# Loading the modulation's shift and scale apart, opening qkv by contraction block, one transpose by DMA, and a new instruction order

## The chip, the cores and the metric

The kernel runs on one NeuronCore of one Trainium2 chip. The metric is device time in microseconds (us) of that core, from runs without other load. A run's time is about 1.7 us longer than the profiled span of the same run, because the span counts from the first instruction to the last.

## The reference, cut

One transformer block whose two layer norms are scaled, shifted and gated by a conditioning vector. S = 2048 tokens, D = 512, 32 heads of 16, bf16.

```python
mod = (_silu(c) @ w_mod).reshape(c.shape[0], 6, 1, -1)
sa, ca, ga, sb, cb, gb = (mod[:, 0].copy(), ..., mod[:, 5].copy())   # 512 numbers each
h = _layernorm(x, axis=-1) * (1 + ca) + sa
x = x + ga * _A_ref(h, A_wqkv, A_wo)          # dilated local attention: window 8, dilation 2
h = _layernorm(x, axis=-1) * (1 + cb) + sb
x = x + gb * _B_ref(h, B_w_gate, B_w_up, B_w_down)   # gelu(h Wg) * (h Wu) @ Wd, Df = 1792
```

`w_mod` is 512 x 3072: its first 512 columns make the shift `sa`, the next 512 the scale `ca`. Nothing of the first qkv product can be computed before both are known.

## The kernel before

Every operation is first recorded in a plan, with its engine and its dependences. The plan is then emitted in one fixed order, the list `ORDER`, which was found beforehand by annealing on a model of the engines. So each engine runs its instructions in exactly that order: an operation whose input is late holds up everything behind it on its engine. Tokens go in five groups of 256, 256, 512, 512 and 512.

The loads that come first, and the two columns of the modulation. The 1 MB load brings shift (`b = 0`) and scale (`b2 = 1`) in one piece:

```python
    load_x(0, 2, -1000)
    load_cols(wm01, w_mod, 0, 2 * D, -999)          # shift and scale, 1 MB, one DMA
    load_cols(wqkv[0], A_wqkv, 0, D, -998)
    ...
        pe(0.41, lambda: cols(b, 0), r=[wm[b] or wm01, scT], w=[(mps, 0)], pri=p)     # shift: 16 matmuls of one column
        pe(0.41, lambda: cols(b2, 1), r=[wm[b2] or wm01, scT], w=[(mps, 1)], pri=p)   # scale
        act(0.09, lambda: nc.scalar.add(out=scl[:, off // 2:off // 2 + 4], in_=mps[:, 4:8], add=1.0), ...)
        act(0.09, lambda: nc.scalar.copy(out=modT[:, off:off + 4], in_=mps[:, 0:4]), ...)
```

Until the first qkv product can start, TensorE is kept busy with dummy matmuls on a tile named `warm` (14 of `warm_up`, then `filler`). How many `filler` matmuls go in is worked out from the gaps that the plan's model sees, so an edit can change their number (7 to 19 in these runs). The norm's output `xn` is transposed on TensorE into `tp` in PSUM, and ScalarE or VectorE applies scale and shift on the way to `hT` (the affine step). Where the tags are `None`, a DMA transpose writes the tile and ScalarE works on it in place:

```python
    LN1_TAGS = (("psL", "psB"), ("psF", "psF"), ("psF", "psF"), None, None)
    LN2_TAGS = (("psB", "psB"), None, None, None, None)
    ...
        if tags is None:
            ...  dq.dma_start_transpose(out=dst[...], in_=xn[...])      # one DMA for two token tiles
            for dt in range(DT):
                act(..., nc.scalar.activation(out=dst[:, 0:n // P, dt, :], in_=dst[:, 0:n // P, dt, :],
                    func=ACT.Identity, scale=scl[...], bias=modT[...]), ...)
```

The qkv product of one output tile, with the four contraction blocks `dt` innermost; the first tile waits for all of `hT[0]`:

```python
            def mm(b=b, j0=j0, ps=ps):
                for j in range(j0, j0 + nj):
                    for dt in range(DT):
                        nc.tensor.matmul(ps[:, j - j0, :], lhsT=wqkv[b][:, dt, j:D:4], rhs=h_cols(hT, g, dt),
                                         start=(dt == 0), stop=(dt == DT - 1))
```

The sums over a head's 16 dimensions and over the window ("folds", tiles `LT` and `o_ps`, `tile_position=(0, 32 * r)`), and the softmax sums `ss`, use the array in four column tiles; qkv, projection (`x_ps`), gate, up and down products (`g_ps`, `u_ps`, `y_ps`) use all of it. And the very last token tile is evicted in two halves, so that the last store is short:

```python
            parts = 2 if g == NG - 1 and c4 == n // P - 1 else 1
```

## Time and profile before

| | before |
|---|---|
| time, median (lowest to highest) | 246.88 us (246.49 to 247.17) |
| profiled span | 244.9 us |
| TensorE busy share | 97% |
| VectorE, ScalarE busy share | 67%, 62% |
| first qkv matmul starts | 13.34 us |
| first qkv tile and second group's transposes done | 14.66 us |
| last matmul ends | 241.44 us |

The last three rows cut the span into what happens before TensorE's real work is under way, the work itself, and the tail. They are read from TensorE's timeline. The prediction below shows the lines of the page, the stretches and the timeline that they come from.

How the views are read: a timeline or chain line begins with start and length in us, then the engine, the line of the kernel and the operation; `xN` counts instructions run together, and brackets hold the idle time before them and what ended it. A line of the waits view ends with total us, times, longest.

### The profile page before, as it was taken

The numbers are of one execution on the slowest core, as the hardware profiler recorded it, in microseconds if no ns is written. First come the engines' busy times: TensorE is split into PE (matmuls) and PEld (weight loads), VectorE is DVE, ScalarE is ACT, GpSimd is POOL, SyncE is SP. The second block draws the span as 40 slices with busy tenths as digits, with TensorE's granted clock in tenths as the row PEclk, the third lists the DMA queues.
The fourth block names the chain that finished last, engine by engine and source line by source line (L and its number), as shares of the span: only waits on it lengthen the run. The fifth ranks groups of instructions, "written<-read, shape, count | busy, mean of one in ns | idle before, by whom it ended". The sixth has DMA issues, their size and how long they took to land.

```text
span 244.9 us, 4342 instructions
## 1 busy us (share of the span) xinstructions
PE 237.5 (97%) x1691; PEld 129.1 (53%) x1691; DVE 164.8 (67%) x317; ACT 152.6 (62%) x280; POOL 22.2 (9%) x45
## 2 busy tenths in 40 slices
PE   7899999999999999999999999999999999999994
PEld 2489755457766534785444444444444444444452
DVE  3999999999995899799876746793432432121222
ACT  2089778988969729883657797157556816657300
POOL 1562012320000200110000001200000110000000
PEclk9999999999999999999999999999999999999998
DMA  6997979999799047592025090410000241000001
GB/s 188 355 305 209 186 180 288 183 248 361 234 215 217 0 131 170 141 220 43 1 60 138 0 186 12 86 64 2 3 0 0 43 88 66 0 0 0 3 24 62
DMA packets 37386, 28.84 MB, mean 118 GB/s; under 512 B 13045, under 2 KB 35958, under 8 KB 37366
## 3 DMA queue, kind: packets, MB, share of 16 engines
q1 hardware_dynamic: 37216, 28.56, 47.3%
q8 instruction: 13, 0.21, 0.4%
q14 instruction: 7, 0.06, 0.1%
q10 hardware_dynamic: 150, 0.00, 0.0%
HBM read 21.40 MB, written 4.28 MB: 105 GB/s over the span
## 4 chain that ended last, share of the span: by engine, by line
PE 79%; DVE 15%; POOL 2%; DMA 1%; issue 1%; ACT 1%; DVEq 0%; POOLq 0%
PE g_ps L786 20%; PE u_ps L786 19%; PE y_ps L813 17%; PE qkv_ps L598 10%; PE x_ps L763 6%; DVE pq L646 4%; DVE st L512 3%; PE o_ps L748 3%; DVE pv L732 3%; PE LT L656 2%; POOL rstd L518 2%; DVE xn L522 2%; DMA x_sg<-in_A_x_dram 1%; PE LT L686 1%; DVE mv L514 1%
## 5 line engine op out<-in xcount | busy, mean ns | idle before, releaser
L786 PE MATMUL g_ps<-h2T,Wg 128*128 128x512 bf16 (+1 forms) x280 | 54.4, 337 | 0.0
L786 PE MATMUL u_ps<-h2T,Wu 128*128 128x512 bf16 (+1 forms) x280 | 54.2, 337 | 0.0
L813 PE MATMUL y_ps<-WdP,hht 128*128 128x512 bf16 (+1 forms) x238 | 49.9, 367 | 0.5 <-DVE hht L798 0.5
L598 PE MATMUL qkv_ps<-hT,wqkv 128*128 128x512 bf16 (+1 forms) x240 | 45.7, 337 | 0.4 <-ACT hT L561 0.4
L795 ACT ACTIVATE gl<-g_ps 128x512 bf16<-128x512 f32 x56 | 33.0, 600 | 18.6 <-PE g_ps L786 17.3
L798 DVE TENSOR_TENSOR hht<-gl,ub 128x512 bf16<-128x512 bf16 x56 | 22.6, 422 | 32.4 <-ACT gl L795 20.4
L797 ACT CAST ub<-u_ps 128x512 bf16<-128x512 f32 x56 | 32.1, 590 | 12.8 <-PE u_ps L786 12.2
L786 PEld LDWEIGHTS <-Wg 128*128 128x128 bf16 x280 | 27.1, 98 | 22.9 <-issue 1.3
L786 PEld LDWEIGHTS <-Wu 128*128 128x128 bf16 x280 | 27.1, 98 | 22.1 <-issue 0.6
L813 PEld LDWEIGHTS <-hht 128*128 128x128 bf16 x238 | 23.1, 98 | 25.7 <-DVE hht L798 0.9
L598 PEld LDWEIGHTS <-wqkv 128*128 128x128 bf16 x240 | 25.7, 114 | 14.2 <-issue 2.2
L518 POOL TENSOR_TENSOR rstd<-rstd,neghalf 128x2 f32<-128x2 f32 x16 | 16.4, 1042 | 173.4 <-DVE rstd L507 143.3
L640 DVE TENSOR_TENSOR pq<-qT,kT 128x2048 bf16<-128x2048 bf16 x24 | 28.6, 1220 | 0.4
L732 DVE TENSOR_TENSOR pv<-e,vR 128x2048 bf16<-128x2048 bf16 x24 | 28.7, 1219 | 0.2
L534 ACT ACTIVATE h2T<-h2T,modT,scl 128x512 bf16<-128x512 bf16 (+1 forms) x16 | 11.1, 753 | 14.1 <-DMA h2T<-xn 14.1
L826 DVE TENSOR_TENSOR ot<-y_ps,x_sg 128x512 bf16<-128x512 f32 (+1 forms) x13 | 8.2, 648 | 14.5 <-PE y_ps L813 13.1
L763 PE MATMUL x_ps<-woP,oT 128*128 128x512 bf16 x64 | 15.8, 380 | 0.0
L767 DVE SCALAR_TENSOR_TENSOR x_sg<-x_ps,x_sg 128x512 bf16<-128x512 f32 x16 | 11.0, 685 | 6.3 <-PE x_ps L763 6.2
L504 ACT ACTIVATE xn<-x_sg,xsum 128x512 bf16<-128x512 bf16 x16 | 11.4, 718 | 3.3 <-DVE xsum L501 3.3
L512 DVE BATCH_NORM_STATS2 st<-x_sg 128x6 f32<-128x512 bf16 x16 | 10.3, 671 | 2.6 <-DMA x_sg<-in_A_x_dram 2.6
L754 ACT CAST oT<-o_ps 128x512 bf16<-128x512 f32 x16 | 9.0, 588 | 4.8 <-PE o_ps L748 4.8
L605 ACT CAST vT<-qkv_ps 128x512 bf16<-128x512 f32 x16 | 9.5, 592 | 3.7 <-PE qkv_ps L598 2.5
(92 smaller groups left out, 203.8 us busy)
## 6 DMA issues: line engine op xcount, KB each, us to landing
vR<-scr SPq DMA_DIRECT2D x24, 260.0 KB, 5.0
vR<-scr SPq DMA_DIRECT2D x8, 264.0 KB, 4.6
wm<-in_w_mod_dram SPq DMA_DIRECT2D x4, 512.0 KB, 5.2
out_dram<-ot SPq DMA_DIRECT2D x15, 128.0 KB, 1.7
Wg<-in_B_w_gate_dram SPq DMA_DIRECT2D x2, 896.0 KB
Wu<-in_B_w_up_dram SPq DMA_DIRECT2D x2, 896.0 KB, 8.1
WdP<-in_B_w_down_dram SPq DMA_DIRECT2D x2, 896.0 KB, 9.9
scr<-vT SPq DMA_DIRECT2D x6, 264.0 KB, 9.6
```

The source lines that it names most:

```text
L504: act(0.75, lambda i=i, xn=xn, nm=nm, mv=mv, c0=c0: nc.scalar.activation(out=xn[:, i, :], in_=x[g, c0 + i], func=ACT.Square, bias=nm[:, i: ...
L512: dve(0.59, lambda i=i, st=st, c0=c0: nc.vector.bn_stats(out=st[:, i, :], in_=x[g, c0 + i]), r=[x.key(g, c0 + i)], w=[(st, i)], pri=p)
L518: gp(0.65, lambda rstd=rstd: nc.gpsimd.tensor_tensor(out=rstd[:], in0=rstd[:], in1=neghalf[:, 0:2], op=ALU.pow), r=[rstd, neghalf], w=[rst ...
L598: nc.tensor.matmul(ps[:, j - j0, :], lhsT=wqkv[b][:, dt, j:D:4], rhs=h_cols(hT, g, dt), start=(dt == 0), stop=(dt == DT - 1))
L640: dve(1.14, lambda j=j, wg=wg, t=pq[m]: nc.vector.tensor_tensor(out=t[:], in0=_ap(q[g][:, j, 0:n], [[0, 4], [1, n]]), in1=_ap(k[g][:, j, : ...
L732: dve(1.14, lambda jj=jj, jl=jl, wg=wg, t=pv[m]: nc.vector.tensor_tensor(out=t[:], in0=_ap(e[:, wg, :], [[0, 4], [1, n]]), in1=vR[g][jj][: ...
L763: nc.tensor.matmul(x1_ps[:], lhsT=oT[:, j, c4 * P:(c4 + 1) * P], rhs=woP[:, j, :], start=(j == 0), stop=(j == 3))
L786: nc.tensor.matmul(ps[:, ft - f0, :], lhsT=Wt[ft // 7][:, dt, ft % 7 * P:(ft % 7 + 1) * P], rhs=h_cols(h2, g, dt), start=(dt == 0), stop=( ...
L795: act(0.485, lambda gl=gl, ps=gu[0]: nc.scalar.activation(out=gl[:], in_=ps[:], func=ACT.Gelu_apprx_tanh), r=[gu[0]], w=[gl], pri=p, table ...
L797: act(0.475, lambda ub=ub, ps=gu[1]: nc.scalar.copy(out=ub[:], in_=ps[:]), r=[gu[1]], w=[ub], pri=p)
L798: dve(0.335, lambda gl=gl, ub=ub, ht=ht: nc.vector.tensor_tensor(out=ht[:], in0=gl[:], in1=ub[:], op=ALU.mult), r=[gl, ub], w=[ht], pri=p)
L813: nc.tensor.matmul(y_ps[:], lhsT=hh[ft // nf][:, ft % nf, c4 * P:(c4 + 1) * P], rhs=WdP[:, ft, c0:c0 + w], start=(ft == 0), stop=(ft == FT ...
```

## The change

Its intent is to start the real work of TensorE sooner and to take a little work off it.

- The 1 MB load is split in two DMAs of 0.5 MB, scale first, so that scale's columns are done while shift still flies.
- The first qkv tile becomes four operations, one per contraction block, in the order in which the blocks of `hT` become ready (2, 0, 3, 1).
- The second norm of the first group is transposed by DMA and no longer by eight TensorE transposes.
- The order list is a new one, annealed over eight perturbed models and with a higher latency for GpSimd.
- Small things go with it: in the plan the dummies no longer wait for `tp` and `modT`, their tile `warm_ps` has another PSUM tag, and `c_cols` is tied to the operation before it (this last line is left out below). Apart from the tag these lines change only the plan, that is, which orders it allows and how many dummies it puts in.

```diff
 ORDER = [
-    5, 8, 0, 1, 55, 7, 9, 41, 42, 39, 40, 43, 44, 54, 45, 6, 32, 33, 4, 15, 34, 46, 47, 264, 12, 136, 10, 134, 262,
+    55, 5, 0, 7, 8, 9, 42, 43, 40, 41, 2, 6, 13, 33, 34, 44, 45, 137, 139, 16, 275, 138, 140, 10, 46, 141, 35, 36, 37,
 ... (the whole list is another; cut)
-        lat = {"pe": 0.2, "act": 0.13, "dve": 0.12, "pool": 0.15, "sp": 0.0}[eng] if lat is None else lat
+        lat = {"pe": 0.2, "act": 0.13, "dve": 0.12, "pool": 0.45, "sp": 0.0}[eng] if lat is None else lat
+    FIRST = (2, 0, 3, 1)
-    LN2_TAGS = (("psB", "psB"), None, None, None, None)
+    LN2_TAGS = (None, None, None, None, None)
-    load_cols(wm01, w_mod, 0, 2 * D, -999)
+    for b in (1, 0):
+        dma(524e3, lambda dq, b=b: dq.dma_start(
+            out=wm01[:, :, b * D:(b + 1) * D], in_=w_mod[:, b * D:(b + 1) * D].rearrange("(t p) n -> p t n", p=P)),
+            w=[(wm01, b)], pri=-999.5 + 0.5 * (1 - b), bw=340e3)
-    wps = T("psF", [P, SG], F32, "warm_ps")
+    wps = T("psL", [P, SG], F32, "warm_ps", "warm")
-        pe(0.41, lambda: cols(b, 0), r=[wm[b] or wm01, scT], w=[(mps, 0)], pri=p)
-        pe(0.41, lambda: cols(b2, 1), r=[wm[b2] or wm01, scT], w=[(mps, 1)], pri=p)
+        pe(0.41, lambda: cols(b2, 1), r=[wm[b2] or (wm01, 1), scT], w=[(mps, 1)], pri=p)
         act(0.09, ... scl ...)
+        pe(0.41, lambda: cols(b, 0), r=[wm[b] or (wm01, 0), scT], w=[mps], pri=p)
         act(0.09, ... modT ...)
-                pl.cold = pe(0.66, filler, r=[warm, tp, modT, scl], w=[wps], pri=-960)
+                pl.cold = pe(0.66, filler, r=[warm, scl], w=[wps], pri=-960)
-            pe(0.866, mm, r=[wqkv[b], hT[g]] + ..., w=[ps], pri=p, after=() if g else [pl.first] if step else [pl.cold])
             if g == 0 and step == 0:
+                for dt in FIRST:      # start flag on the first matmul of the bank only, stop on its last
+                    pe(0.22, lambda mm=mm, dt=dt: mm((dt,)), r=[wqkv[b], (hT[g], dt)] + ..., w=[ps], pri=p, after=[pl.cold])
+            else:
+                pe(0.866, lambda mm=mm: mm(range(DT)), r=[wqkv[b], hT[g]], w=[ps], pri=p, after=() if g else [pl.first])
```

## The prediction

> **What bounds the kernel now.** I read the page's busy table and slices first, then the stretches table by stage, then the chain of waits in order of time, then the timeline of the first 15 us, and last the instruction order of both programs, which the change rewrites.
>
> The busy table and the slices:
>
> ```profile
> span 244.9 us, 4342 instructions
> ...
> PE 237.5 (97%) x1691; PEld 129.1 (53%) x1691; DVE 164.8 (67%) x317; ACT 152.6 (62%) x280; POOL 22.2 (9%) x45
> ```
>
> TensorE is busy nearly throughout; no other engine is over 67%. But busy does not mean useful: 31 of its matmuls (14 and 17, lines of `warm_ps`) are dummies that keep it warm before real work can start. The stretches table separates the two (columns: stretch, its length, busy time and count of each engine, clock, DMA share, GB/s):
>
> ```profile
> 0.00:13.30 13.30, 10.51 (x75) 4.82 (x76) 8.73 (x28) 2.81 (x6) 5.34 (x22) 1.00 0.83 278
> 13.30:30.00 16.70, 16.66 (x172) 14.42 (x171) 15.82 (x32) 13.79 (x25) 4.78 (x13) 1.00 0.96 225
> 30.00:60.00 30.00, 29.56 (x318) 17.64 (x317) 29.28 (x55) 25.04 (x49) 5.40 (x4) 1.00 1.01 248
> 60.00:120.00 60.00, 59.31 (x500) 36.84 (x498) 53.95 (x89) 45.07 (x82) 2.95 (x3) 1.00 0.62 147
> 120.00:180.00 60.00, 60.00 (x336) 26.38 (x335) 38.89 (x71) 37.41 (x68) 2.35 (x2) 1.00 0.25 56
> 180.00:241.50 61.50, 61.42 (x299) 28.99 (x297) 17.74 (x46) 28.49 (x54) 1.38 (x2) 1.00 0.11 25
> ```
>
> From 13.3 to 241.5 us TensorE is idle for only 0.04 + 0.44 + 0.69 + 0.00 + 0.08 = 1.25 us. So three things set the end: when the first qkv matmul starts, how much TensorE work follows it, and a fixed tail of 3.4 us (last eviction and output transfer). What holds the first qkv back is in the timeline (start, length, engine, line, what, count, idle before it):
>
> ```profile
> 8.11 2.75 PE L436 MATMUL warm_ps<-warm 128*128 128x512 bf16 x12
> 10.70 0.54 PE L458 MATMUL modT_ps<-scT,wm 128*128 128x1 bf16 x16
> 11.49 0.54 PE L458 MATMUL modT_ps<-scT,wm 128*128 128x1 bf16 x16 [0.25 <-ACT modT L465]
> 11.89 1.02 PE L436 MATMUL warm_ps<-warm 128*128 128x512 bf16 x4
> 13.34 1.03 PE L598 MATMUL qkv_ps<-hT,wqkv 128*128 128x256 bf16 x8 [0.43 <-ACT hT L561]
> 14.21 0.61 PE L546 MATMUL tp<-ident,xn 128*128 128x128 bf16 x8
> 14.66 0.27 PE L598 MATMUL qkv_ps<-hT,wqkv 128*128 128x256 bf16 x1
> ```
>
> The reader sees dummies until the 1 MB piece of w_mod lands (about 10.4), then shift columns, then scale columns after a 0.25 us wait on the PSUM tile that ScalarE still reads, then dummies while the affine step makes hT. ScalarE makes two of its four blocks one after the other (1.02 us from 12.27), and the first qkv group waits for all four.
>
> **What the Trainium skill says.** "DMA: Bandwidth & Descriptors", section "Specifications", gives 512 B as the smallest transfer that keeps line rate. The split turns 2 KB runs of w_mod into 1 KB runs, so it should cost little. The trace agrees roughly: 370 to 377 GB/s around 9 to 11 us, mainly the 2 KB runs, and 346 to 349 around 12 to 14 us, mainly 1 KB runs. "PSUM — Partial Sum Buffer", section "The four PSUM rules", says that the matmul that opens an accumulation clears the written-bits of the whole bank, and that two groups open at once in one bank cannot both open it. The two halves of the first qkv tile share a bank and are now interleaved, so only the first matmul of all carries the start flag. That is correctness, not time. "TensorE: Matmul & The Clock Gate", section "Part 4: PE-mode transpose", gives about 275 ns for a 128x128 transpose in a kernel. This trace disagrees for a stream of them: the chain gives four of them 0.22 us, 55 ns each, so I use 55 ns.
>
> **The change part by part.**
>
> Shift and scale apart. The bytes ahead of the last half of this piece are the same in both programs (three x loads, 1 MB, then w_mod), so shift lands where the whole did, about 10.4 us. Scale, 0.5 MB ahead of it at some 370 GB/s, lands 1.4 us sooner, and its 0.54 us of columns and its eviction leave the path. From shift: columns 10.70 to 11.24, eviction of 0.16 to 11.44, affine step from about 11.5 instead of 12.27. That is 0.8 us.
>
> First qkv by contraction block, order 2, 0, 3, 1. VectorE makes blocks 2 and 3 (0.73 us for two, from the row at 12.27), ScalarE 0 and 1 (1.02). Blocks are then ready at about 11.9 (2), 12.0 (0), 12.4 (3), 12.5 (1). TensorE stands behind 3 dummies (0.65) and the first four transposes of the second group (0.22), thus about 12.1. Blocks 2, 0 and 3 take 0.22 to 0.26 each and end about 12.85; four more transposes to 13.1; block 1 to 13.3. At that time the first qkv group and all eight transposes of the second group are done. In the kernel before the same work was done at 14.66. Saving of the opening: 14.66 − 13.3 = 1.36 us. The 0.8 above is contained in it.
>
> First second-norm transposes by DMA. Eight PE transposes go: two pieces of 0.22 us in the chain, 0.45 us of TensorE. In their place comes one DMA transpose; the seven that the kernel already has for h2T land 3.1 us (median) after issue. It is on the path only if h2T is late.
>
> The new order. The instruction lists show 32 switches between column-tiled matmuls (folds, softmax sums) and full ones after the first qkv, and 28 in the changed program. The chain shows what a switch costs:
>
> ```profile
> 40.07 0.99 PE o_ps L748 x32
> 41.07 0.99 PE qkv_ps L598 x4
> ...
> 51.77 0.86 PE qkv_ps L598 x4
> ```
>
> The same four qkv matmuls take 0.99 just after a fold and 0.86 otherwise: 0.12 to 0.13 a switch. Four fewer save 0.5 us. All other TensorE work is the same matmuls in another order. The 1.25 us of idle can only shrink to zero or grow; I leave it.
>
> Sum: 1.36 + 0.45 + 0.5 = 2.3 us. 246.88 − 2.3 = 244.6 us.
>
> **Rivals.**
>
> A: the DMA transpose makes a new wait. TensorE's order is fixed, so if h2T of the first group is late, the first gate matmul stalls everything behind it. In the kernel before the last projection of that group ended at 44.34, and xn was ready at 50.99 (rows of VectorE at 50.25, 0.74 long): 6.65 us. Add 3.1 us, or the 5.2 us that the hT transposes take in the same crowded stretch, and four affine steps of about 0.6: 12.2 to 14.3 us. By the instruction list, with 0.216 us for each 512-column matmul, the changed program puts about 16 us of TensorE work between that projection and the first gate matmul (13.4 before). So it fits, with 2 to 4 us to spare. Against that: transfers are at their densest there (share 1.38 in 44 to 52 us), and wqkv needed 10.2 us to land early on. A landing of 10 us would stall about 3 us and give 247.5. The up-weights also stand behind this transpose in the SP queue; their 1.8 MB at 335 GB/s need 5.5 us, and there is as much TensorE work ahead of their use.
>
> B: the opening is bound by something else, and its saving shrinks. The changed program needs the second group's normalised rows before its first qkv, and gives VectorE three more statistics (0.6 each) before the first normalisation. By the durations of the rows before, the first rows are normalised at about 8.8 and the second group's at 11.4, both before their use, but the second with only half a microsecond to spare. If it fails, the opening saves 0.6 and the result is 245.4.
>
> C: the annealed order also removes the remaining idle, or finds more. At most 1.25 us are there to be had: 243.4. A gain over 2% (under 241.94) would need 4.9 us, and the three savings and all of the idle come to 3.6. The idle may also grow, since every wait in the middle is new.
>
> **Range and chances.** The centre is the sum with a little of C: 244.5. The low end, 243.3, is C in full. The high end, 246.2, is B with a small stall of kind A. Faster by over 2% needs a saving that no view shows: 0.02. Slower by over 2% needs over 7 us of new stalls in a fixed order: 0.02. Within 2%: 0.96.
>
> **What would show it.** First qkv at about 12.1 and the following qkv group at about 13.3, with about 14 dummies after warm-up counted instead of 17; affine step right behind the shift columns at 11.5; only `tp` groups of the first norm (32 transposes instead of 40); eight DMA transposes of h2T; TensorE idle after the opening 1.2 us or less; last matmul near 239. Wrong if: a wait of TensorE or ScalarE on DMA h2T with an idle TensorE near 60 to 66 us (A); the first qkv later than 12.6 behind VectorE's normalisation (B); scale landing together with shift; or idle of over 2 us spread over the attention stages (the new order).

## The result, and the profile after

| | before | after |
|---|---|---|
| time, median (lowest to highest), us | 246.88 (246.49 to 247.17) | 244.99 (244.8 to 245.1) |
| profiled span, us | 244.9 | 243.3 |
| first qkv matmul starts | 13.34 | 12.14 |
| first tile and second group's transposes done | 14.66 | 13.26 |
| from there to the end of the last matmul | 226.78 | 226.17 |
| last matmul ends | 241.44 | 239.43 |
| from there to the end of the span | 3.41 | 3.87 |

The ratio of the times is 0.9923, with a 95% interval of 0.9906 to 0.9941. A ratio here is the mean time of one kernel's runs over the mean of the other's runs of the same rounds, so it is not quite the ratio of the medians. The change makes the kernel faster by 0.8%: the interval excludes no change, and the size is well within 2%. On another chip the same two kernels later gave a ratio of 0.9962 (0.9935 to 0.9989) and medians 1.3 us apart instead of 1.9 (c_after below), so the gain is known only to within about half a microsecond. The result is correct.

The busy line on the page of the changed kernel:

```profile
PE 235.3 (97%) x1660; PEld 128.2 (53%) x1680; DVE 163.4 (67%) x317; ACT 148.5 (61%) x278; POOL 25.7 (11%) x45
```

TensorE is still the bound. Compare the two counts of TensorE: 1680 weight loads, but 1660 matmuls. Twenty matmul records are missing from this trace, so its busy sum is too small (223.81 us over the working part, where the complete trace below gives 224.89), and TensorE's idle time must not be read from it. A later run of the very same kernel (the control, below) has all 1680 records; its stretches are used instead. That answers to the stretches table of the kernel before (columns as there; the first stretch begins where that run had finished its first tile and transposes, the last ends with the last matmul):

```profile
13.05:30.00 16.95, 16.95 (x179) 14.20 (x178) 15.22 (x34) 13.37 (x26) 11.03 (x22) 1.00 1.04 258
30.00:60.00 30.00, 29.55 (x275) 15.90 (x273) 28.65 (x51) 25.02 (x48) 4.13 (x3) 1.00 0.99 208
60.00:120.00 60.00, 59.21 (x528) 37.80 (x527) 55.43 (x91) 41.68 (x78) 4.12 (x3) 1.00 0.67 165
120.00:180.00 60.00, 60.00 (x331) 26.57 (x329) 38.26 (x72) 38.82 (x74) 1.73 (x2) 1.00 0.25 54
180.00:239.20 59.20, 59.19 (x289) 27.99 (x286) 16.60 (x42) 25.83 (x48) 1.41 (x2) 1.00 0.10 27
```

TensorE is idle for 0.00 + 0.45 + 0.79 + 0.00 + 0.01 = 1.25 us and busy for 224.89. The kernel before, over the same part of its run (14.66 to 241.44), is busy for 225.63 and idle for 1.15.

The opening, in the timeline of the changed kernel (TensorE's groups, and the affine step on ScalarE):

```profile
9.13 0.55 PE L462 MATMUL modT_ps<-scT,wm 128*128 128x1 bf16 x16 [0.36 <-DMA wm<-in_w_mod_dram]
...
10.62 0.55 PE L462 MATMUL modT_ps<-scT,wm 128*128 128x1 bf16 x16
...
11.41 2.86 ACT L565 ACTIVATE hT<-tp,modT,scl 128x256 bf16<-128x256 bf16 x6
11.68 0.39 PE L550 MATMUL tp<-ident,xn 128*128 128x128 bf16 x4
12.14 0.84 PE L607 MATMUL qkv_ps<-hT,wqkv 128*128 128x256 bf16 x6
12.82 0.39 PE L550 MATMUL tp<-ident,xn 128*128 128x128 bf16 x4
13.05 0.38 PE L607 MATMUL qkv_ps<-hT,wqkv 128*128 128x256 bf16 x2
13.26 2.46 PE L603 MATMUL qkv_ps<-hT,wqkv 128*128 128x256 bf16 x21
```

Scale's columns now run 1.49 us ahead of shift's. The affine step begins at 11.41 instead of 12.27, and six matmuls of the first tile (blocks 2, 0, 3) run before its last block is needed. The tile and the eight transposes of the second group are through at 13.26, 1.40 us sooner.

What TensorE still waits for in the middle, in the waits of the changed kernel (a third one is `u_ps` for ScalarE's `gl`, 0.3):

```profile
PE x_ps L777 <- DVE rinv L723: 0.5, 1, 0.5
PE LT L700 <- DVE m L695: 0.4, 1, 0.4
```

The kernel before waited there for other things (`y_ps` for VectorE's `hht` 0.5, `LT` for `pq` 0.4, `o_ps` for `pv` 0.2). The new order has exchanged these waits rather than removed them (the second of them goes away in the old order too: see b_both).

The end. VectorE's timeline, the last eviction of the kernel before:

```profile
241.46 0.42 DVE L826 TENSOR_TENSOR ot<-y_ps,x_sg 128x256 bf16<-128x256 f32 x1 [0.72 <-PE y_ps L813]
```

and the last ones of the changed kernel:

```profile
237.94 0.76 DVE L840 TENSOR_TENSOR ot<-y_ps,x_sg 128x256 bf16<-128x256 f32 x2 [2.57 <-PE y_ps L827]
239.45 0.69 DVE L840 TENSOR_TENSOR ot<-y_ps,x_sg 128x512 bf16<-128x512 f32 x1 [0.76 <-PE y_ps L827]
```

Before, the half-width tile comes last (0.42 us to evict, 64 KB to store). In the new order the two halves come second to last, and a full tile ends the program (0.69 us, 128 KB). The tail grows from 3.41 to 3.87 us.

So the span's 1.55 us is −1.40 (opening) − 0.61 (work) + 0.46 (tail). The experiments ask which part of the change carries each of these.

### The profile page after: what moved, and what is told of

The parts are those of the page before. It is cut to its first block, busy times and chain, and to the rows that moved or that the text cites. A ratio compares the mean times of both kernels' runs of the same rounds, so it can differ in the third digit from the quotient of the medians.

```text
span 243.3 us, 4304 instructions
## 1 busy us (share of the span) xinstructions
PE 235.3 (97%) x1660; PEld 128.2 (53%) x1680; DVE 163.4 (67%) x317; ACT 148.5 (61%) x278; POOL 25.7 (11%) x45
## 4 chain that ended last, share of the span: by engine, by line
PE 70%; DVE 17%; DMA 5%; issue 2%; POOL 2%; ACT 2%; DVEq 0%; ACTq 0%; POOLq 0%
PE y_ps L827 20%; PE u_ps L800 20%; PE g_ps L800 19%; PE x_ps L777 4%; DVE pq L654 4%; DMA wqkv<-in_A_wqkv_dram 3%; DVE pq L660 3%; DVE pv L752 3%; PE o_ps L762 2%; POOL rstd L522 2%; DVE st L516 2%; PE LT L670 2%; PE qkv_ps L603 1%; DVE xn L526 1%; DMA x_sg<-in_A_x_dram 1%
## 5 line engine op out<-in xcount | busy, mean ns | idle before, releaser
L827 PE MATMUL y_ps<-WdP,hht 128*128 128x512 bf16 (+1 forms) x230 | 49.1, 366 | 0.4
L603 PE MATMUL qkv_ps<-hT,wqkv 128*128 128x512 bf16 (+1 forms) x229 | 43.7, 339 | 0.1
L811 ACT CAST ub<-u_ps 128x512 bf16<-128x512 f32 x56 | 31.7, 589 | 14.9 <-PE u_ps L800 11.7
L522 POOL TENSOR_TENSOR rstd<-rstd,neghalf 128x2 f32<-128x2 f32 x16 | 17.5, 1094 | 162.4 <-DVE rstd L511 140.1
L603 PEld LDWEIGHTS <-wqkv 128*128 128x128 bf16 x232 | 24.9, 114 | 13.6 <-issue 1.3
L538 ACT ACTIVATE h2T<-h2T,modT,scl 128x512 bf16<-128x512 bf16 (+1 forms) x20 | 13.2, 726 | 15.1 <-DMA h2T<-xn 15.1
L777 PE MATMUL x_ps<-woP,oT 128*128 128x512 bf16 x57 | 14.9, 379 | 0.7 <-DVE rinv L723 0.5
L508 ACT ACTIVATE xn<-x_sg,xsum 128x512 bf16<-128x512 bf16 x16 | 11.5, 721 | 4.3 <-DVE xsum L505 4.3
L619 ACT CAST kT<-qkv_ps 128x512 bf16<-128x512 f32 x16 | 9.5, 602 | 1.8 <-PE qkv_ps L603 1.8
L619 ACT CAST qT<-qkv_ps 128x512 bf16<-128x512 f32 x16 | 9.5, 600 | 1.3 <-PE qkv_ps L603 1.3
```

What stands on the lines that cost most here:

```text
L522: gp(0.65, lambda rstd=rstd: nc.gpsimd.tensor_tensor(out=rstd[:], in0=rstd[:], in1=neghalf[:, 0:2], op=ALU.pow), r=[rstd, neghalf], w=[rst ...
L619: act(0.475, lambda t=t, off=off, j0=j0, ps=ps: nc.scalar.copy(out=t[:, j0:j0 + nj, off:off + n], in_=ps[:]), r=[ps], w=[(t, j) for j in r ...
L777: nc.tensor.matmul(x1_ps[:], lhsT=oT[:, j, c4 * P:(c4 + 1) * P], rhs=woP[:, j, :], start=(j == 0), stop=(j == 3))
L811: act(0.475, lambda ub=ub, ps=gu[1]: nc.scalar.copy(out=ub[:], in_=ps[:]), r=[gu[1]], w=[ub], pri=p)
L827: nc.tensor.matmul(y_ps[:], lhsT=hh[ft // nf][:, ft % nf, c4 * P:(c4 + 1) * P], rhs=WdP[:, ft, c0:c0 + w], start=(ft == 0), stop=(ft == FT ...
```

## The experiments

The theories that they had to separate. Theory 1: the opening's gain needs the new order; the split load and the blocks save little without it, and the DMA transpose is only safe with it. Theory 2, the rival: the parts are worth their own amounts in any order and simply add up. Separate questions were what a switch between column-tiled and full matmuls costs, and whether the tail's growth is the order's doing.

There were twelve runs in three calls. Each call had its own chip and its own runs of the kernel before: medians 246.47 (runs named b), 246.46 (a) and 246.48 (c). Names with b start from the kernel before, names with a and c from the changed kernel. All twelve gave correct results. The call of the a runs had no run of the changed kernel in it. "The new order" stands below for all that b_both lacks in the opening: the list `ORDER` together with the small things named above. No run parts these.

| run | median us | ratio to before [95%] |
|---|---|---|
| b_split | 246.15 | 0.9988 [0.9965, 1.0012] |
| b_blocks | 245.90 | 0.9980 [0.9964, 0.9996] |
| b_both | 245.51 | 0.9985 [0.9947, 1.0023] |
| b_ln2dma | 248.76 | 1.0103 [1.0071, 1.0136] |
| a_merge | 245.79 | 0.9974 [0.9963, 0.9986] |
| a_noblocks | 245.03 | 0.9946 [0.9934, 0.9958] |
| a_turns | 248.02 | 1.0066 [1.0054, 1.0078] |
| a_tail | 245.47 | 0.9965 [0.9949, 0.9982] |
| c_after | 245.16 | 0.9962 [0.9935, 0.9989] |
| c_tail | 244.47 | 0.9931 [0.9912, 0.9950] |
| c_better | 244.04 | 0.9903 [0.9890, 0.9916] |
| c_x4late | 247.36 | 1.0038 [1.0025, 1.0051] |

Some kernels had single runs 1 to 3 us above their others (b_both 248.71 and 246.84 among four of 245.4 to 245.6). These pull the means, hence the ratios, more than the medians. Where the two disagree, I use the timeline, which shows the edited place itself.

### b_split: the split load alone

```diff
-    load_cols(wm01, w_mod, 0, 2 * D, -999)
+    for b in (1, 0): dma(524e3, ... wm01[:, :, b * D:(b + 1) * D] ...)     # and scale's columns first, as in the change
```

> The kernel before with one part alone: shift and scale load apart, scale first. Theory 1 (the new order carries the opening): shift's affine step starts near 11.5 us instead of 12.27 and the first qkv starts near 12.5 instead of 13.34, but the eight transposes of the second group still stand behind it and wait for VectorE's normalised rows, which were ready at 13.8; so the qkv group after them starts only 0.3 us sooner (14.35 instead of 14.66) and the time falls by 0.3 us. Theory 2 (the parts add up): the qkv group after them starts 0.8 us sooner and the time falls by 0.8 us.

Measured: 246.15 us, 0.3 under before, not clear of noise. In its timeline the first tile and transposes are done at 14.20 (before 14.66), 0.46 us sooner. Shift's columns run from 10.47, but the tile starts only at 12.33, behind ScalarE's two blocks (11.26 to 12.28), and VectorE comes to its two blocks only at 12.10. The second group's rows are normalised from 12.95 on, so the transposes run at 13.74. The six times fall into two groups (245.4 to 245.7 and 246.6 to 247.1); the profile is of the first.

### b_blocks: the blocks alone

```diff
-            pe(0.866, mm, r=[wqkv[b], hT[g]] + ..., w=[ps], ...)
+                for dt in FIRST:
+                    pe(0.22, lambda mm=mm, dt=dt: mm((dt,)), r=[wqkv[b], (hT[g], dt)] + ..., w=[ps], ...)
```

> The kernel before with the first qkv tile computed block by block of the contraction, alone. First qkv from about 12.7 us, its last two matmuls behind ScalarE's second affine step (13.29), end 13.56. Theory 1: the transposes behind it again wait for the normalised rows at 13.8, so the next qkv group starts at about 14.35 and the time falls by 0.3 us. Theory 2: 0.65 us.

Measured: 245.90 us. The first qkv matmul starts at 12.84 instead of 13.34, but the tile's last six matmuls wait 0.22 us more, and tile and transposes are done at 14.54. That is 0.12 us sooner (0.21 if one allows for shift's columns, which ran 0.09 later in this run). Here the earlier start of the tile gained little, since its last block set its end. The run as a whole gained more than that: its last matmul ended at 240.91, 0.53 us sooner than before, and the interval excludes no change. Where the rest came from is said under b_both.

### b_both: split and blocks, old order

The edit is the two above together.

> The kernel before with both parts of the opening but the old order. Theory 1: still 0.3 to 0.4 us, since the normalised rows of the second group (13.8 us) set when the next qkv group starts; TensorE idles near 13 to 13.8. Theory 2: 1.3 to 1.4 us, as in the changed kernel, where the next qkv group starts at 13.26.

Measured: median 245.51, nearly 1 us under before; the mean has the outliers named above and its interval includes no change. The timeline of this run, TensorE's groups and VectorE's:

```profile
12.58 1.03 PE L615 MATMUL qkv_ps<-hT,wqkv 128*128 128x256 bf16 x8 [0.86 <-DVE hT L568]
12.96 1.94 DVE L534 TENSOR_SCALAR xn<-x_sg,mv,rstd 128x512 bf16<-128x512 bf16 x5
13.76 0.62 PE L558 MATMUL tp<-ident,xn 128*128 128x128 bf16 x8
14.21 1.58 PE L611 MATMUL qkv_ps<-hT,wqkv 128*128 128x256 bf16 x13
```

Shift's columns are as early as in the changed kernel (10.50). Still the tile waits 0.86 us for VectorE's `hT` blocks, and the second group's rows are normalised only from 12.96, so its transposes run at 13.76, behind the tile. They are done at 14.21, as with the split alone. That is theory 1 for the opening: the other 0.95 us of it (14.21 to 13.26) comes only with the new order, which puts the second group's normalised rows and transposes ahead of the tile's last block, where before there were dummies. The total (median −1.0) came out better than the opening shows (−0.45): this run's last matmul ended at 240.33, so 0.66 us more were gained further on. The stretches show where. TensorE's idle time over the working part fell from 1.15 to 0.71 and its busy time from 225.63 to 225.41. The busy time's 0.22 stays open. The idle time is one wait of the kernel before:

```profile
31.59 0.62 PE L656 MATMUL LT<-pq,Mph 128*32 128x256 bf16 x16 [0.44 <-DVE pq L646]
```

It is gone in b_split, b_blocks and b_both, and with it a wait of 0.36 us of VectorE for GpSimd at 14.9. Both waits are still there in b_ln2dma, whose opening is unchanged. GpSimd's own times are nearly the same in all five, so why VectorE no longer waits stays open.

This changes how the whole change is to be judged. From the end of the opening to the last matmul b_both takes 226.12 us and the changed kernel 226.15: with the DMA transpose and fewer switches TensorE is busy for 0.52 us less (224.89), but it is idle for 0.54 us more. So by the profiles b_both, with the old order, already has 1.2 us (span 243.7) of the 1.6 us; the new order adds 0.95 in the opening and loses 0.5 in the tail.

### b_ln2dma: the DMA transpose alone, old order

```diff
-    LN2_TAGS = (("psB", "psB"), None, None, None, None)
+    LN2_TAGS = (None, None, None, None, None)
```

> The kernel before with the first second-norm transposes by DMA alone, old order. TensorE has 0.45 us less to do. If the transpose is hidden the time falls by 0.45 us. If the old order leaves it too little room (xn ready 51.0, 3 to 5 us to land, four affine steps of 0.6: 56.4 to 58.4 against the first gate matmul at 57.0, which would now come at 56.6), the first gate matmul waits up to 2 us and the time rises by 0 to 1.5 us.

Measured: 248.76 us, 2.3 us slower, worse than expected. In its timeline:

```profile
50.96 2.91 SPq L529 DMA_TRANSPOSE h2T<-xn  x1
...
55.93 1.09 ACT L534 ACTIVATE h2T<-h2T,modT,scl 128x256 bf16<-128x256 bf16 x2 [4.59 <-DMA h2T<-xn]
...
57.55 1.02 PE L598 MATMUL qkv_ps<-hT,wqkv 128*128 128x512 bf16 x4 [1.85 <-ACT vT L605]
...
59.99 0.71 PE L786 MATMUL g_ps<-h2T,Wg 128*128 128x256 bf16 x5 [1.09 <-ACT h2T L534]
```

The transpose is issued at 50.96 and its first affine step starts at 55.93. ScalarE stands at that step for 4.59 us. Behind it, in ScalarE's queue, is the eviction of a `vT` tile that has nothing to do with this norm, and TensorE waits 1.85 us for the PSUM bank that this eviction frees, then 1.09 us for `h2T` itself. The Trainium skill, "Perfetto Trace Analysis", section "Tensor Engine Instruction (MATMUL, LD_WEIGHTS)", says that the execution queues of ScalarE, VectorE and GpSimd are strictly first in, first out. This trace agrees: one late DMA holds an unrelated eviction. The two waits, 2.9 us, less the 0.45 us of transposes saved, come to 2.5, near the measured 2.3.

The new order keeps clear of this. The changed kernel's lines for the same tile:

```profile
58.93 1.27 SPq L533 DMA_TRANSPOSE h2T<-xn  x1
62.52 0.62 ACT L538 ACTIVATE h2T<-h2T,modT,scl 128x256 bf16<-128x256 bf16 x1
...
67.30 0.93 PE L800 MATMUL g_ps<-h2T,Wg 128*128 128x256 bf16 x7
```

The affine step (three more instructions, left out) ends at 66.06 and the first gate matmul starts at 67.30 without a wait: a margin of 1.2 us. Theory 2 is wrong for this part: alone it costs 2.3 us, and within the new order nothing of that is paid.

### a_merge: the changed kernel with one transfer for shift and scale

```diff
-    for b in (1, 0): dma(524e3, ... wm01[:, :, b * D:(b + 1) * D] ...)
+    load_cols(wm01, w_mod, 0, 2 * D, -999)
```

> The changed kernel with shift and scale again in one transfer, all else as changed. TensorE's order puts the scale columns ahead of the first-group transposes, so with scale landing at 10.4 instead of 9.1 those transposes, 0.45 us, and the dummies fall behind it: shift columns at about 11.7 instead of 10.62, next qkv group at about 14.3 instead of 13.26. Time up by 1.0 us. If the split is not what opens it, less than 0.3 us.

Measured: 245.79 us, 0.8 above the changed kernel's own median, and 0.76 above a_noblocks, with ratios whose intervals do not overlap. Scale's columns start at 10.84 and shift's at 11.68, and tile and transposes are done at 14.05 instead of 13.26, where the next qkv group starts:

```profile
14.05 1.15 PE L600 MATMUL qkv_ps<-hT,wqkv 128*128 128x256 bf16 x9
```

That is 0.79 us in the timeline too. But not all of it need be the split's. The 1 MB load had landed at 10.20, 7.8 us after its issue at 2.35, while TensorE was in dummies, of which the plan put in 19 here and 14 in the changed kernel:

```profile
8.68 2.32 PE L437 MATMUL warm_ps<-warm 128*128 128x512 bf16 x10
10.84 0.54 PE L459 MATMUL modT_ps<-scT,wm 128*128 128x1 bf16 x16
```

In the changed kernel the columns of each half start 0.05 us after it has landed (9.08 and 9.13, 10.57 and 10.62); here they start 0.64 us after. So some 0.6 of the 0.79 us may be dummies that the plan had put in for a later landing, and what is left for the split itself in the new order is about 0.2 us (an estimate from these times). No run has one load and fewer dummies, so this rival is untested. In the old order the split gave 0.46 in the opening, fewer dummies (14 for 17) included.

The kernel before has the same gap. Its load is issued at 2.37, the last number of this line of its DMA view is the time in us to landing, and so it landed at 10.0, while the columns start at 10.70:

```profile
wm<-in_w_mod_dram SPq DMA_DIRECT2D x1, 1024.0 KB, 7.6
```

### a_noblocks: the changed kernel with the first tile in one piece

The edit is b_blocks reversed.

> The changed kernel with the first qkv tile again in one piece. Theory 1 (order and split carry the opening): TensorE does both sets of second-group transposes while it waits; ScalarE's last affine step still ends at 12.45, the tile runs 12.5 to 13.4, and the qkv group after it starts 0.1 to 0.2 us later than 13.26: time up by 0.1 to 0.2 us. If the blocks carry as much as the prediction's list made of them, it rises by 0.5 us or more.

Measured: 245.03 us, the changed kernel had 244.99. The tile starts later, but all eight transposes of the second group are done before it:

```profile
11.71 0.61 PE L549 MATMUL tp<-ident,xn 128*128 128x128 bf16 x8
...
12.38 2.81 PE L601 MATMUL qkv_ps<-hT,wqkv 128*128 128x256 bf16 x24
```

At 0.11 us each, its eight matmuls end at about 13.25 (an estimate, since the row runs on into the next groups), where the changed kernel's end (13.26). In the new order the blocks are worth nothing that can be measured: TensorE does the same work in the other sequence.

### a_turns: more switches between column-tiled and full matmuls

In `ORDER`, folds and full matmuls of two stretches are alternated: 42 switches instead of 28, the same matmuls.

```diff
 ORDER: 644 moved behind 559, 766 behind 560, 634 behind 551, 603 behind 552, 858 behind 788, 883 behind 789,
        838 behind 778, 857 behind 779, 827 behind 780
```

> The changed kernel with nine matmul groups moved in TensorE's order so that column-tiled folds and full matmuls alternate: 42 switches after the opening instead of 28, no other change. If a switch costs the 0.115 us that the rows show, the time rises by 14 x 0.115 = 1.6 us. If the longer rows at a switch are only how starts are recorded, it stays at 245.0 (up to 0.4 for later folds).

Measured: 248.02 us, 3.0 above the changed kernel, in the median and in the span (246.3 against 243.3). The cost of a switch shows in the chain of waits, where nothing waits for anything:

```profile
164.23 0.33 PE o_ps L762 x4
164.56 0.97 PE u_ps L800 x4
```

and, for comparison, in the chain of the changed kernel:

```profile
119.60 0.86 PE u_ps L800 x4
...
129.10 0.98 PE o_ps L762 x16
130.08 0.97 PE u_ps L800 x4
```

Four up matmuls take 0.97 just after a fold and 0.86 elsewhere; four folds take 0.33 just after a full matmul, where sixteen in a row take 0.98 with one switch among them. So a switch costs 0.11 to 0.12 us either way. Eight of the added ones lie in one stretch, from the folds at 162.10 (changed kernel) or 164.23 (this run) to the next projection at 169.45 or 172.46: the same matmuls take 7.35 us there and 8.23 here, 0.88 more. The Trainium skill, "TensorEngine Tiling (Array Packing)", section "Key Properties", says that changing the tiling mode drains TensorE, without a figure; the trace agrees that a change costs time and gives the figure, but does not show that it is a drain. Fourteen switches make 1.5 to 1.7 us. The other 1.3 to 1.5 us I had not expected. The moved folds finish the second `oT` tile later, and ScalarE stands 1.58 us (until 133.05) for it. The exponentials are behind that eviction in ScalarE's queue and start at 134.95 instead of 132.50, and TensorE then waits for them near 136 us (`ss` for `e`, 0.7 us in the waits). From 120 to 160 us TensorE is idle for 0.84 us here and not at all in the control. That part is read from the trace and was not isolated, and some 0.5 us is left without a cause.

### a_tail and c_tail: the half-width tile last again

The last 31 operations of `ORDER` are rearranged so that the half-width eviction and store end the program. Nothing else moves. The same kernel ran twice.

```diff
-    ..., 998, 987, 988, 995, 996, 997, 1010, 989, 990, 991, 1011, 999, 1004, 1005, 1012, 1006, 1007, 1013, 1008, 1014, 1015, 1000, 1001, 1009, 1002, 1003
+    ..., 998, 987, 988, 995, 996, 997, 999, 989, 990, 991, 1000, 1001, 1002, 1003, 1004, 1005, 1006, 1010, 1007, 1008, 1009, 1011, 1012, 1013, 1014, 1015
```

> The changed kernel, only its last 31 operations put in another order, so that the half-width tile of the last output chunk is evicted and stored last, as in the kernel before, and not a full tile. If the tail after the last matmul (3.87 us in the changed kernel, 3.41 before) grew because of that order, it goes back to about 3.4 and the time falls by 0.4 us to 244.6. If the longer tail is chance, the time stays at 245.0.

Measured: span 243.0, of which the tail after the last matmul is 3.44 us, as expected. The times said nothing: three runs at 244.7 to 245.0 and three at 245.9 to 246.2. So it was run again with a control beside it.

> The tail order of a_tail again, because that run gave two groups of times (244.7 to 245.0 and 245.9 to 246.2) while its profile had the tail at 3.44 us. If the second group is an accident of that chip, this run is 0.4 us under the changed kernel. If the new tail order itself causes it, two groups about 1 us apart appear again and the mean is no better.

Measured: 244.47 us against the control's 245.16; span 242.7 against 243.1, last matmul at 239.30, tail 3.4 us. The slow group did not come back, but for one run of 246.03 at a granted clock of 0.991. The tail's 0.46 us is the order's doing and can be had back. The times agree in sign and size (−0.7) but the two ratios' intervals overlap; the profile is what shows it.

### c_after: the changed kernel again, as control

No edit.

> The changed kernel itself, unchanged, as the measure for the three others of this call and for the scatter between chips: 245.0, ratio to the kernel before 0.992 to 0.995.

Measured: 245.16 us, ratio 0.9962, so the expected ratio (0.992 to 0.995) was missed. Two runs of six are at 246.7 and 246.8 at a clock of 0.99. The other four are at 244.6 to 245.3, where the changed kernel was before. Its opening was through at 13.05 instead of 13.26, since the halves of the modulation landed some 0.2 us sooner: shift's columns at 10.42 instead of 10.62. So 0.2 us of the opening is scatter of the loads.

### c_better: the tail mended and two waits avoided

The tail of c_tail, and two neighbours on TensorE exchanged where the waits view named a wait: one qkv product goes ahead of the projection that waited for `rinv`, one ahead of the `LT` update that waited for the maximum.

```diff
 ORDER: tail as in c_tail; 500 moved ahead of 121; 719 moved ahead of 346
```

> The changed kernel with the tail order and two swaps of neighbours in TensorE's order: a qkv group ahead of the second output projection of the first group, which waited 0.5 us at 49 for VectorE to free its PSUM buffer, and a qkv group ahead of the max subtraction, which waited 0.45 us at 65.5 for VectorE. If those waits cost the end, the time is 1.2 us under the changed kernel: tail 0.4, swaps 0.8. If the work behind is held by VectorE anyway, the swaps give nothing and only the 0.4 us of the tail come.

Measured: 244.04 us (243.95 to 244.21), 1.1 under the control and 2.4 under the kernel before, the fastest of all. In the waits of its trace those of 0.5 and 0.4 us are gone, `u_ps` for `gl` is still there (0.3), and a new one came (`LT` for `pq`, 0.2). The last matmul ended at 238.88, 0.31 before the control's, and the tail is back at 3.4 us: the spans (242.3 against 243.1) differ by these two. The profiled runs themselves, at 244.78 and 244.04, are 0.74 apart; the other 0.3 us of the medians is scatter. The waits named in the profile were thus real, though about a third of their sum is what reached the end: TensorE's idle time fell by 0.60 (1.25 to 0.65), but its busy time rose by 0.29 (224.89 to 225.18). Why it rose is open.

### c_x4late: a later load of later rows

A try at the opening's new limit. The rows of the third group are loaded behind the first qkv weights, and their statistics move behind the affine step, so that shift and scale land sooner.

```diff
 ORDER: 16 moved behind 12; 275, 273, 265, 267, 274 moved behind 54
```

> The changed kernel with the 0.5 MB of x rows for the third group loaded behind the first qkv weights instead of ahead of w_mod, and their four statistics moved behind the first affine step on VectorE. Shift and the first weights land 1.4 us sooner, the first qkv starts near 10.7 instead of 12.1. If the opening alone is the limit, the time falls by 1.2 to 1.4 us. If VectorE, busy over 90% from 13 to 60 us, is what the attention stages wait for, its statistics now come 2.4 us of work later, TensorE stands still later on and the gain is under 0.4 us or negative.

Measured: 247.36 us, 2.2 above the control. The first qkv matmul came at 11.26, 0.67 us sooner than in the control (11.93), about half of what was hoped. But TensorE then waited 0.9 us for the next qkv weights, 1.4 for VectorE's `pq`, which comes behind the moved statistics in VectorE's order, and 1.1 for the up weights. (The profiled run, 248.77, is the slowest of the six; the waits may be a little shorter in the others.) From 8 to 14 us the DMA engines and VectorE of the changed kernel are about as full as TensorE (DMA share 1.07 to 1.12; VectorE busy 5.16 of 6 us, TensorE 5.47), and in this run what one load gained the next ones lost.

## Why the prediction was right, and where it was not

The time, 244.99, is 0.5 us above the centre, and 0.4 above the sum. Some of this closeness is luck. In the profiles the predicted 2.3 us came out as 1.55: the opening gave 0.04 more than the prediction has, the work 0.34 less, and the tail took 0.46. The medians fell by 1.89 because the profiled run of the kernel before (246.59) lay 0.3 under its median; in the control's call they fell by 1.3. By its steps:

- **What bounds the kernel**: right. TensorE's work runs without a gap of more than 0.5 us, and the difference is opening plus work plus tail.
- **The opening, −1.36 us**: right in size, −1.40. The details came as said: affine step at 11.41 (predicted about 11.5), first qkv at 12.14 (12.1), 14 dummies after the warm-up (14, by weight loads; one of their matmul records is missing). By its own durations block 3 would be ready at 12.2 and not at 12.4; it was ready at 12.29, without effect on the end. The split's share, 0.8 us, is what a_merge measured, but up to 0.6 of that may be dummies. The prediction took the landing of the 1 MB load (about 10.4) from the start of the columns behind it; it landed at 10.0, and TensorE stood in dummies for 0.7 us more (a_merge). That the columns of shift came at 10.62 as reckoned (10.70), behind a half that landed at 10.57, is luck. In the old order VectorE was not ready for its two blocks before 12.24 in any case; what fewer dummies alone would give was not run. The rest was credited to the wrong part. The prediction presents the 0.56 us beside the 0.8 under the contraction blocks; a_noblocks shows that these give nothing in the new order, and b_both that blocks and split together without it leave 0.95 us undone. It is the new order, which does the second group's transposes in time that dummies had filled.
- **Transposes and switches, −0.95 us**: direction right, size a third short. In complete traces TensorE's busy time fell by 0.74 us (225.63 to 224.89) and its idle time rose by 0.10 (1.15 to 1.25), which together make 0.63 (226.78 to 226.15). The switch price of 0.12 held in a_turns, the switches are 32 and 28 in the traces too, and all 32 remaining transposes belong to the first norm. Which of the two terms is short by 0.2 us is open: no run takes the DMA transpose or the four switches alone out of the changed kernel.
- **The idle time, left as it was**: right, 1.25 against "1.2 or less", but its members changed, and two of them were avoidable (c_better). Against b_both, which has 0.71, the new order has made it worse.
- **The tail, "a fixed tail of 3.4 us"**: this step failed. The tail was 3.87, because the new order ends with a full tile. The prediction read the order on TensorE for switches and not on VectorE and the store queue for the end. This 0.46 us is the largest single miss, ahead of the work's 0.3.
- **Rival A, the DMA transpose**: rightly held to be the main danger, and rightly said to be hidden, but the margin is 1.2 us rather than 2 to 4. Its harm without the order went another way than described: less by the gate matmul's own wait (1.09) than by an eviction stuck behind the affine step (1.85).
- **Rival B**: did not come, but only just: the second group's rows were normalised at 11.58 (predicted 11.4) and their transposes started at 11.68, so 0.1 us was to spare where half a microsecond had been reckoned.
- **Rival C**, less idle: did not come by itself; about 0.3 us of it was to be had by two exchanges.
- **Two readings beside the sum.** The prediction put 346 to 349 GB/s down to the 1 KB runs. In the changed kernel, where shift and scale come in 1 KB runs, the rate is 380 and 376 GB/s from 8 to 10 us (399 and 377 before) and 345 from 10 to 11, so the shorter runs cost little, and the lower rate has another cause, which no run shows. And the skill's 275 ns is how long one transpose lasts, while the prediction's 55 ns is how far apart the starts are: single records here last 219 ns. The two do not contradict each other; 55 ns was the right one to count with.

## What to carry to other kernels

In a kernel whose busiest engine never rests, add up three terms: when its real work begins, how much there is, and what comes after its last instruction; and check the third in the new instruction order too, on the engine and the queue that end the program. A part of a change may be worth nothing or do harm without the order that goes with it, so try each part both alone on the old kernel and taken away from the new one. Where a model puts in filler work ahead of a load, compare when the load lands with when its reader starts. Where a DMA feeds an engine that runs strictly in order, ask what unrelated work stands behind that step.

## What the Trainium skill lacked or had wrong

- "TensorEngine Tiling (Array Packing)", section "Key Properties", says that a change of tiling mode drains TensorE but gives no cost. Here a switch costs 0.11 to 0.12 us in either direction (four matmuls in 0.97 us instead of 0.86; eight switches 0.88 us).
- "TensorE: Matmul & The Clock Gate", section "Part 4: PE-mode transpose", gives about 275 ns for a transpose in a kernel, but not what one adds in a stream of them. Here one record lasts 219 ns, and in a stream each 128x128 transpose adds 55 ns (four in 0.22 us).
- "DMA: Bandwidth & Descriptors", section "DMA Transpose (X-bar)", has no time from issue to landing for a transpose from SBUF to SBUF. For 256 KB it was 3.1 us in the median of the changed kernel's `h2T` transposes, and 5.0 us passed from issue to first use in the crowded stretch of b_ln2dma (50.96 to 55.93).
